# Other loads, fold engines and order for the first stage of an FFT-and-MLP kernel

## The chip, the cores and the metric

The kernel runs on one core of a Trainium2 chip. The metric is the device time of one execution in microseconds (us), and a kernel's time is the median of several runs. Profiles come from one more execution, recorded by the hardware profiler; their times count from the start of its span.

## The reference

The input x has 8 batches of 3008 rows of 256 columns, in f32. Each batch goes through a Fourier transform over its rows and one over its columns, and the real part is kept. The resulting 24064 rows are then the tokens of a two-layer MLP with a hard-swish between its layers:

```python
X = np.fft.fft(x, axis=1)              # (8, 3008, 256)
X = np.fft.fft(X, axis=2).real.astype(np.float32)
t = X.reshape(24064, 256)
h = t @ w_in                           # 256 x 2048
g = h * np.clip(h + 3.0, 0.0, 6.0) / 6.0
out = g @ w_out                        # 2048 x 256
```

## The kernel before

**The work and its stages.** The transform over 3008 = 47 x 64 rows is done in two stages of matrix products with constant tables, 47 points (table `F`) and 64 points (table `T`). The column transform is a table `C`, which is folded into `w_in` (the products of L860), so that it costs no stage of its own. Then come the two products of the MLP: L566 gives `u` and `v`, ScalarE and VectorE make the hard-swish of them (L575 to L617), and L641 and L661 multiply by `w_out` and gather the sums `acc`. L724 to L727 (`send`) store the result. The batches run one behind the other in an order fixed by hand: the program is recorded under a manual schedule, so each engine's queue holds its instructions in the order of the source. The body of the kernel is a long sequence in which stage one and two of the next batches are threaded between the MLP products of this one; the change does not touch it, apart from which moment the first pieces of it begin.

**Stage one of the first batch.** This is the part that the change rewrites. It has no MLP work beside it, since nothing has been transformed yet. It runs in four units, m = 0, 1, 3, 2 (`FIRST`), and each unit in two parts. Part 0 works on a forward tile `hb.x[m]`, part 1 on a reverse tile `hb.xr[m]`. A tile has 128 partitions of 4 consecutive rows of x (4 x 256 f32, 4 KB a partition), so 512 KB; 47 + 47 of the partitions hold what is computed on, the halves starting at partitions 0 and 64 (`PB` = 64, `XC` = 4). In both kernels the reverse tiles are read by an indirect gather on GpSimd's queue (L175), by a list of row numbers that `iota` makes; in the kernel before, so are the forward tiles, the two kinds in turn.

Each part is first folded, since a real transform over columns needs only sums and differences of a column and its mirror: columns 129 to 255 of `y` become differences (L203), columns 1 to 127 sums (L212), and columns 0 and 128 are copied (L209 on ScalarE, L214 on VectorE). TensorE then multiplies `y` by the table in four quarters (two halves of rows by two of columns, 47x512, L347 and, one slot at a time, L352), and the middle column of the raw tile by two more tables (`unit_middle`, L335). In the kernel before, part 0 of the first two units is different: TensorE sums near and far columns itself, in products of 258 and 254 columns from the raw tile (`unit_by_pe`), and VectorE makes only the differences (`sine`). A unit's sums are copied out of PSUM (`evict_first`, L365 to L367), sent to a scratch array `zd` in DRAM, and read back regrouped for stage two (L447, `g<-zd`).

**The weights.** `w_in` and `w_out` come in pieces of 512 KB (`load_w`, L769 to L774): the pieces 0 and 1 are of `w_in`, 2 and 3 are of `w_out`, and so on in turn. Each piece j is taken apart on chip into a scaled form by `exponent_a` (ScalarE, L790), `exponent_b` (TensorE, L804), `exponent_c` (ScalarE, L807), `mantissa` (VectorE, L815 and L816) and `join` (VectorE, L824 and L830). `fold_w_in` then multiplies a piece of `w_in` by `C` (L860), copies it out, and `send_wn` (L847) sends part of it through DRAM.

**Order around the start, before.** SyncE's queue holds the table `FI` and piece 0. ScalarE's holds `F`, `first_slot` (48 partitions of 1 KB, for the one slot that has no row of its own) and, after the first unit, piece 1. GpSimd's holds the eight gathers, `C`, two tables `T` and pieces 2 and 3. `exponent_a` and `mantissa` of piece 0 stand ahead of the units on their engines, its `exponent_b` and `exponent_c` behind the first unit's part 0. `keep_awake` (L887) issues filler products of 128x512 on constants, four of them before the first tile.

The stores of `send` serve as a comparison in the prediction. Their DRAM side is written in three dimensions, `rows[:, q].rearrange("b i e -> i b e")`, and their SBUF side is the tile `o` with 128 partitions.

Of the kernel before, what the change touches and what calls it, by code (L numbers as in the profile page):

```python
# [58 lines left out]
def kernel(  # L59
# [10 lines left out]
    nc = tc.nc  # L70
# [108 lines left out]

    class Half:  # L180
# [20 lines left out]
    def fold_columns(x, y, part, js, eng):  # L201
        far, near = x[0:PX - 1, js, D - 1:P:-1], x[0:PX - 1, js, 1:P]
        eng.tensor_tensor(y[:, js, P + 1:D], *((far, near) if part else (near, far)), op=AL.subtract)  # L203
        return near, far

    def fold_all(x, part, eng, steps=(slice(0, XC),), copy=None):
        y = ypool.tile([PX - 1, XC + 1, D], F32, tag="y", name="y")
        if copy:
            copy(y[:, 0:XC, 0:P + 1:P], x[0:PX - 1, :, 0:P + 1:P])  # L209
        for js in steps:  # L210
            near, far = fold_columns(x, y, part, js, eng)
            eng.tensor_tensor(y[:, js, 1:P], near, far, op=AL.add)  # L212
            if not copy:
                eng.tensor_copy(y[:, js, 0:P + 1:P], x[0:PX - 1, js, 0:P + 1:P])  # L214
        return y
# [116 lines left out]
    def unit_middle(m, part, x, pt, open_, close):  # L332
        for i, h, js, slots, alone in quarters(m, part):
            t = (1 + part) if alone else (5, 7)[part]
            nc.tensor.matmul(pt[h][i * PB:(i + 1) * PB, js], table(t, h), x[rows(h), slots, P:P + 1], start=open_ and not alone, stop=close,  # L335
                             skip_group_check=True)

    def unit_columns(m, part, src, ps, to, fr, open_, close, only=None):
        for i, h, js, slots, alone in quarters(m, part):
            parts = [(to, fr)]  # L340
            if alone and (to.start or 0) <= P < to.stop - 1:
                parts = [(slice(0, P + 1), slice(0, P + 1)), (slice(P + 1, D), slice(P + 1, D))]
            for a, b in parts:
                t = (1 + part + 2 * (a.start > P)) if alone else (0, 6)[part]
                o = ps[h][i * PB:(i + 1) * PB, js, a]
                if only is None:
                    nc.tensor.matmul(o, table(t, h), src[rows(h), slots, b], start=open_ and not alone, stop=close, skip_group_check=True)  # L347
                    continue
                js_, sl = range(js.start, js.stop), range(XC)[slots]
                for jj, ss in zip(js_, sl):  # L350
                    if jj == only:
                        nc.tensor.matmul(ps[h][i * PB:(i + 1) * PB, jj:jj + 1, a], table(t, h), src[rows(h), ss:ss + 1, b],  # L352
                                         start=False, stop=close, skip_group_check=True)

    def unit_by_pe(m, part, x, sine, ps, open_):
        unit_columns(m, part, x, ps, slice(0, P + 1), slice(0, P + 1), open_, False)
        unit_columns(m, part, x, ps, slice(1, P), slice(D - 1, P, -1), False, False)
        unit_columns(m, part, sine, ps, slice(P + 1, D), slice(P + 1, D), False, False)

    def evict_first(hb, m, ps, pt):  # L360
        k = FIRST.index(m)
        pool, tag = ((zpool, "z"), (zpool, "z"), (apool, "a"), (cpool, "c"))[k]
        z = pool.tile([PX, 2, 2, D + 1], F32, tag=tag, name="z")
        for h in range(2):
            nc.scalar.copy(z[:, h, :, D:], pt[h][0:PX])  # L365
        nc.scalar.copy(z[:, 0, :, 0:D], ps[0][0:PX])
        (nc.vector.tensor_copy if k == NM - 1 else nc.scalar.copy)(z[:, 1, :, 0:D], ps[1][0:PX])  # L367
        if not first.zd:
            first.zd[0] = dpool.tile([NG, 2 * KK, 2, NS, D + 1], F32, tag="zd0", name="zd")
        zd = first.zd[0][:].rearrange("g k c (h n) d -> (g k c) h (n d)", h=2)  # L370
        n0 = 2 * 4 * KK
        for i in range(2):
            n = (m * XC + 2 * i) * (D + 1)
            for j in range(PZ // n0):
                dst = zd[j * n0:(j + 1) * n0, :, n:n + 2 * (D + 1)]
                rs = slice(i * PB + j, i * PB + 2 * n0, 2) if j < 2 else slice(i * PB + 2 * n0, i * PB + PZ)
                src = z[rs].rearrange("p h n d -> p h (n d)")
                if j == 0:
                    (nc.scalar if k == NM - 1 and i else nc.sync).dma_start(out=dst, in_=src)
                else:  # L380
                    later.setdefault((j, k), []).append((dst, src))
# [377 lines left out]
    def load_w(j):  # L759
# [5 lines left out]
        if kind == "in":  # L765
            c0, c1 = in_columns(n, i)
            for h, cs in enumerate((slice(c0, c1 + P),) if n else (slice(c0, c0 + P), slice(c1, c1 + P))):
                nf = cs.stop - cs.start
                (nc.sync, nc.scalar, nc.gpsimd)[min(j, 2)].dma_start(  # L769
                                    out=o.rearrange("p (c j) -> p c j", c=2)[:, :, h * P:h * P + nf],  # L770
                                    in_=moe_w_in[:, cs].rearrange("(c p) f -> p c f", p=P))
# [20 lines left out]
    def exponent_b(j, own=False):  # L792
        pm = [PM[j % len(PM)][:, i].bitcast(F16) for i in range(2)]
        if (starting[0] or j == 4) and not own:
# [54 lines left out]
    def fold_w_in(j):  # L849
# [12 lines left out]
        if n == 0:  # L862
            o = W1[:].rearrange("p b (h f) -> p b h f", h=2)[:, :, :, c0:c0 + P]
            nc.vector.tensor_copy(o, ps[:].rearrange("p b (h f) -> p b h f", h=2))
# [18 lines left out]
    def keep_awake(n, ps=None):  # L883
        if ps is None:
            ps = ps_d.tile([P, 2 * TB], F32, tag="d", name="awake")
        for i in range(n):
            nc.tensor.matmul(ps[:], ones[:], Z[:], start=True, stop=True)  # L887
# [11 lines left out]
    for k, m in enumerate(FIRST):  # L899
        take_half(hb, m, *((xpool, "x"), (xpool, "x"), (qpool, "q"), (apool, "a"))[k])  # L900
# [36 lines left out]
    for i in range(2):  # L937
# [11 lines left out]
    for j in range(2, 4):  # L949
        load_w(j)  # L950
    clear_table(0)
    exponent_a(0)
    mantissa(0)
    clear_table(1)
    every = slice(0, D)

    def fold_unit(k, part):
        x = (hb.xr if part else hb.x).pop(FIRST[k])
        if k < 2 and part == 0:
            sine = cpool.tile([PX - 1, XC, D], F32, tag="c", name="sine")  # L960
            fold_columns(x, sine, 0, slice(0, XC), nc.vector)
            return x, sine
        steps = (slice(1, XC, 2), slice(0, XC, 2)) if k == NM - 1 and part else (slice(0, XC),)
        return x, fold_all(x, part, nc.vector, steps, nc.scalar.copy if k > 1 else None)

    unit = fold_unit(0, 0)
    for k, m in enumerate(FIRST):
        ps, pt = first_banks(m)
        x, y = unit
        if k == 0:  # L970
            unit_middle(m, 0, x, pt, True, False)
        if k < 2:
            unit_by_pe(m, 0, x, y, ps, True)
        else:
            unit_columns(m, 0, y, ps, every, every, True, False)
        if k == 0:
            exponent_b(0)
            exponent_c(0)
        else:
            unit_middle(m, 0, x, pt, True, False)  # L980
        x, y = fold_unit(k, 1)
        unit_middle(m, 1, x, pt, False, True)
        if k < NM - 1:
            unit_columns(m, 1, y, ps, every, every, False, True)
            unit = fold_unit(k + 1, 0)
        else:
            for j in range(2):
                unit_columns(m, 1, y, ps, every, every, False, True, only=j)
            join(0)
        evict_first(hb, m, ps, pt)  # L990
        if k == 0:
            nc.scalar.copy(zero_slot(hb), first_slot[PB:PX, 0:D])
            load_w(1)
# [3 lines left out]
    seen = wpool.tile([P, 1], F32, tag="seen", name="seen")  # L997
    mantissa(1)
    fold_w_in(0)
    exponent_a(1)  # L1000
    keep_awake(1)
    exponent_b(1)
    exponent_a(2, (0,))
    exponent_c(1)
    exponent_a(2, (1,))
    join(1)
    mantissa(2)
# [6 lines left out]
    exponent_b(2)  # L1014
    exponent_a(3, (0,))
    exponent_c(2)
    exponent_a(3, (1,))
    mantissa(3)
    fold_w_in(1)
    join(2)  # L1020
    stage2_half(hb, 0)
    exponent_b(3)
    spread_by_pe(hb, bank([P, TB], "ps3")[:])
    tail(3)
# [77 lines left out]
    uv = mlp1_products(*chunk(0))  # L1102
    activate(*chunk(0), *uv)
    ps = spare[0]
# [198 lines left out]
```

## Time and profile before

| | |
|---|---|
| median of 3 runs | 1935.53 us (1935.20 to 1935.71) |
| the profiled execution, its own time | 1933.92 us |
| its span | 1932.2 us |
| mean granted clock of TensorE | 0.997 |
| VectorE, ScalarE, GpSimd busy | 74%, 35%, 75% of the span |
| moved by DMA | 99.03 MB, 51 GB/s over the span |
| DMA in the first 24 us | 56% of 16 engines' time to 4 us, then 98 to 102% |
| L661, the second product of the MLP | 1238.9 us of PE |
| L566, the first product of the MLP | 777.1 us of PE |

PE is TensorE and PEld its weight loads, which lie beside the products. A line of a timeline gives start, length, engine, line of the kernel, operation, output and inputs with their shapes, the count, and in brackets the idle time before it with what ended that. A line of the windows gives, for each engine, the busy time and the number of instructions, then the clock that was granted to TensorE (1.00 is full speed), the share of the 16 DMA engines' time that was used, and GB/s. In the DMA view a queue's line gives packets, MB, and the share of 16 engines. SPq, ACTq and POOLq are the queues by which SyncE, ScalarE and GpSimd issue transfers.

The busy times of L661 and L566 add up to more than the span because products are pipelined and one's record overlaps the next's.

### The profile page before, as it was taken

To read this page: it belongs to the slowest core of one execution; us is meant where nothing else is said; L and a number is where in the kernel's file an instruction comes from. 1 tells how busy PE (TensorE), PEld (TensorE's weight loads), DVE (VectorE), ACT (ScalarE), POOL (GpSimd) and SP (SyncE) were. 2 spreads that over 40 slices of the span, in tenths; PEclk is the share of its full clock that TensorE was granted. 3 is DMA by queue.
4 is the path that set the end of the run, shared out by engine and by line. 5 is a ranking of instruction groups with operands and counts; after the bars stand their busy time and mean duration, and the time that the engine had idled before them with its cause. 6 is when DMAs were issued, how large, how long until landed. Compare 5 with 4: busy or idle time off the path is not lost.

```text
span 1932.2 us, 28221 instructions
## 1 busy us (share of the span) xinstructions
PE 1915.4 (99%) x9354; PEld 1650.8 (85%) x9354; DVE 1425.0 (74%) x2752; ACT 679.3 (35%) x1168; POOL 1442.7 (75%) x1653
## 2 busy tenths in 40 slices
PE   8999999999999999999999999999999999999998
PEld 5688888888988888888898888888899888888887
DVE  6877776677777777777787777777778777777777
ACT  6543333333333333333333333333333333333332
POOL 4597888896688778787678877878666667666765
PEclk9999999999999999999999999999999999999999
DMA  8431232311112222121111221121110101101000
GB/s 286 122 87 49 56 83 72 64 44 38 32 33 67 62 53 55 44 54 34 31 36 50 52 55 44 52 53 50 36 28 20 28 17 27 33 14 28 18 21 20
DMA packets 155592, 99.03 MB, mean 51 GB/s; under 512 B 122163, under 2 KB 137246, under 8 KB 155446
## 3 DMA queue, kind: packets, MB, share of 16 engines
q1 hardware_dynamic: 142582, 57.63, 12.4%
q0 software_dynamic: 11168, 38.51, 6.8%
q8 instruction: 73, 1.20, 0.3%
q10 hardware_dynamic: 1696, 1.10, 0.2%
q14 instruction: 73, 0.60, 0.1%
HBM read 59.87 MB, written 37.32 MB: 50 GB/s over the span
## 4 chain that ended last, share of the span: by engine, by line
PE 96%; DVE 2%; ACT 1%; DMA 0%; issue 0%; another core or an unknown queue 0%; SPq 0%; DVEq 0%; ACTq 0%
PE acc L661 57%; PE v L566 17%; PE u L566 16%; PE ps L514 2%; PE acc L641 1%; PE ps L287 1%; DVE a L617 1%; PE spare L860 1%; DVE s L575 0%; ACT t L614 0%; DVE o L722 0%; PE ps L475 0%; DVE u L598 0%; DMA st<-in_moe_w_in_dram 0%; PE wps L860 0%
## 5 line engine op out<-in xcount | busy, mean ns | idle before, releaser
L631 POOL TENSOR_TENSOR c<-a 128x512 f32<-128x512 f32 (+1 forms) x375 | 469.0, 1251 | 360.3 <-PE acc L661 310.5
L661 PE MATMUL acc<-c,G 128*128 128x256 f32 (+1 forms) x3008 | 697.2, 375 | 0.0
L614 ACT ACTIVATE t<-u,half 128x512 f32<-128x512 f32 (+1 forms) x384 | 260.5, 678 | 1144.2 <-DVE u L585 1062.4
L661 PEld LDWEIGHTS acc<-c,G 128*128 128x128 f32 x3008 | 565.3, 190 | 71.5 <-POOL c L631 0.4
L575 DVE SCALAR_TENSOR_TENSOR s<-qn,WN,u 128x256 f32<-128x256 f32 (+1 forms) x768 | 330.2, 471 | 339.3 <-PE u L566 336.7
L661 PE MATMUL acc<-a,G 128*128 128x256 f32 (+1 forms) x2256 | 541.7, 376 | 0.0
L661 PEld LDWEIGHTS acc<-a,G 128*128 128x128 f32 x2256 | 421.0, 189 | 73.6 <-issue 20.2
L566 PE MATMUL v<-q,W 127*128 127x256 f32 (+1 forms) x1536 | 389.2, 375 | 1.6 <-DVE a L617 1.3
L566 PE MATMUL u<-q,W 128*128 128x256 f32 (+1 forms) x1536 | 387.9, 375 | 0.0
L617 DVE SCALAR_TENSOR_TENSOR a<-t,u 128x512 f32<-128x512 f32 (+2 forms) x448 | 263.9, 601 | 102.5 <-ACT t L614 99.4
L566 PEld LDWEIGHTS v<-q,W 127*128 127x128 f32 x1536 | 287.9, 190 | 42.0 <-ACT t L614 2.2
L566 PEld LDWEIGHTS u<-q,W 128*128 128x128 f32 x1536 | 285.8, 190 | 36.9 <-issue 2.4
L631 POOL TENSOR_TENSOR c<-a,c 128x256 f32<-128x256 f32 (+1 forms) x375 | 268.5, 716 | 29.4
L631 POOL TENSOR_TENSOR c<-c,a 128x256 f32<-128x256 f32 (+1 forms) x375 | 268.4, 716 | 29.4
L585 DVE TENSOR_TENSOR u<-s,v 128x512 f32<-128x512 f32 x352 | 245.0, 696 | 38.1 <-DVE s L575 1.9
L617 DVE SCALAR_TENSOR_TENSOR a<-t,v 128x512 f32<-128x512 f32 (+1 forms) x480 | 263.1, 564 | 0.2
L614 ACT ACTIVATE t<-v,half 128x512 f32<-128x512 f32 (+1 forms) x384 | 260.4, 678 | 0.6 <-issue 0.4
L587 DVE TENSOR_TENSOR v<-v,s 128x512 f32<-128x512 f32 x352 | 243.7, 692 | 0.0
L631 POOL TENSOR_TENSOR r<-w,e 128x256 f32<-128x256 f32 (+1 forms) x92 | 88.8, 986 | 3.6
L671 ACT ACTIVATE e<-acc 128x512 f32<-128x512 f32 (+2 forms) x184 | 83.3, 544 | 0.0
L722 DVE STREAM_TRANSPOSE o<-r 128x256 f32<-128x256 f32 (+1 forms) x192 | 72.5, 414 | 0.2
L631 POOL TENSOR_TENSOR w<-w,e 128x512 f32<-128x512 f32 (+1 forms) x46 | 57.5, 1251 | 3.6
(127 smaller groups left out, 773.2 us busy)
## 6 DMA issues: line engine op xcount, KB each, us to landing
out_dram<-o SPq DMA_DIRECT2D x744, 32.0 KB
g<-zd SPq DMA_DIRECT2D x42, 256.0 KB
zd<-z SPq DMA_DIRECT2D x48, 192.0 KB
xt<-in_x_dram POOLq DMA_DIRECT2D x21, 256.0 KB, 3.7
st<-in_moe_w_out_dram POOLq DMA_DIRECT2D x8, 512.0 KB, 6.6
qn<-qd SPq DMA_DIRECT2D x16, 256.0 KB
xt<-in_x_dram POOLq DMA_DIRECT2D x17, 192.0 KB, 4.0
st<-in_moe_w_in_dram POOLq DMA_DIRECT2D x6, 512.0 KB, 4.9
```

Source lines behind the costliest of these rows:

```text
L287: nc.tensor.matmul(ps[b][h * PB:(h + 1) * PB, 0:n], F[rows(b), 0:PB], y[rows(b), 2 * h:2 * h + n], start=True, stop=not last, skip_group_c ...
L514: nc.tensor.matmul(ps[:, blk, u * P:n].rearrange("p (b k) -> p b k", b=2), g[:, kk, blk * (P + 1):blk * (P + 1) + P], T[:, :, gr, blk, kk, ...
L566: nc.tensor.matmul(ps[:, i, 0:nq], W1[r, blk, f * P:(f + 1) * P], q[r, blk, of:of + nq], start=True, stop=True)
L575: nc.vector.scalar_tensor_tensor(s[:, i, 0:nq], qn[:, of:of + nq], WN[:, f:f + 1], u[:, i, 0:nq], op0=AL.mult, op1=AL.add)
L585: nc.vector.tensor_tensor(u[:], s[:], v[:], op=AL.add)
L587: nc.vector.tensor_tensor(v[:], v[:], s[:], op=AL.subtract)
L614: nc.scalar.activation(t, h, AF.Relu, bias=half[:], scale=scale)
L617: nc.vector.scalar_tensor_tensor(dst, t, 1.0, h, op0=AL.min, op1=AL.mult)
L631: (eng or nc.gpsimd).tensor_tensor(out, in0, in1, op=AL.add)
L661: nc.tensor.matmul(ch.acc[i // 2][:, i % 2, 0:ch.n], G[:, i, fc, :], mv, start=(fc == 0 and i % 2 == 0), stop=(fc == NF - 1), skip_group_c ...
L671: nc.scalar.mul(ch.e[:, k:i + 1, 0:ch.n], ch.acc[i // 2][:, 0:i + 1 - k, 0:ch.n], 1.0 / WS)
L722: nc.vector.transpose(o[:, 0:n // DH, h], ch.r[:, m, h, 0:n].rearrange("p (j i) -> p j i", i=DH))
```

## The change

- The four forward tiles of the first batch are no longer gathered. `load_rows` issues each as one plain load on SyncE's queue, ahead of all else on it. Its source is the 64 partitions' worth of rows of `x_pn` with one more dimension of two ahead of it, for the second half of the tile.
- Pieces 0 and 1 of the weights follow on the same queue. `FI` moves to ScalarE's queue, between `F` and `first_slot`. GpSimd's queue begins with the four reverse gathers.
- All units are folded alike (`fold_unit`), and `unit_by_pe` is gone. The differences of part 0 of units 1, 2 and 3 are taken by GpSimd. Pieces 2 and 3 are issued on GpSimd's queue behind the second of these.
- A filler product of 128 columns stands behind each of the first seven parts.
- The copies out of unit k - 1 stand behind part 0 of unit k, for the last of them within part 1 of the last unit, behind `exponent_a` of piece 0. The wider half of a copy out goes to VectorE for two units instead of one.
- `mantissa`, `exponent_b`, `exponent_c` and `join` of piece 0 move behind stage one. `fold_w_in(1)` and the `exponent_b`, `exponent_c` and `join` of piece 3 move behind the first `u` and `v`. Some of the filler products between them are moved or made narrower.

The core of the diff:

```diff
+    def load_rows(o, m, queue):
+        a = x_pn[0:PB, m * XC + 1:(m + 1) * XC + 1, :].rearrange("p n d -> p (n d)")
+        queue.dma_start(out=o[:].rearrange("p n d -> p (n d)"),
+                        in_=bass.AP(a.tensor, a.offset, [[NM * XC * D, 2], *a.ap]))
...
+    def fold_unit(x, part, steps=(slice(0, XC),), copy=nc.scalar.copy, sine=nc.vector):
         y = ypool.tile([PX - 1, XC + 1, D], F32, tag="y", name="y")
...
+            copy(y[:, js, 0:P + 1:P], x[0:n, js, 0:P + 1:P])
+            far, near = x[0:n, js, D - 1:P:-1], x[0:n, js, 1:P]
+            sine.tensor_tensor(y[:, js, P + 1:D], *((far, near) if part else (near, far)), op=AL.subtract)
+            nc.vector.tensor_tensor(y[:, js, 1:P], near, far, op=AL.add)
...
     keep_awake(4)
+    keep_awake(1, TB)
     hb = halves[0]
-    nc.sync.dma_start(out=FI[:], in_=c_stage1[:, 13 * PB:])
-    load_w(0)
+    for k, m in enumerate(FIRST):
+        take_half(hb, m, *((xpool, "x"), (xpool, "x"), (qpool, "q"), (apool, "a"))[k])
+        load_rows(hb.x[m], m, nc.sync)
+    for j in range(2):
+        load_w(j)
     nc.scalar.dma_start(out=F[:], in_=c_stage1[:, 0:8 * PB])
+    nc.scalar.dma_start(out=FI[:], in_=c_stage1[:, 13 * PB:])
...
-        if i == 0:
-            gather(hb.x[FIRST[0]], IT[:, NM + FIRST[0]:NM + FIRST[0] + 1], P, D)
-    for m in FIRST:
-        if m != FIRST[0]:
-            gather(hb.x[m], IT[:, NM + m:NM + m + 1], P, D)
-        gather(hb.xr[m], IT[:, m:m + 1], P)
+        if i:
+            for m in FIRST:
+                gather(hb.xr[m], IT[:, m:m + 1], P)
...
     for k, m in enumerate(FIRST):
         ps, pt = first_banks(m)
-        x, y = unit
...
+        end = k == NM - 1
+        for part, tiles in enumerate((hb.x, hb.xr)):
+            x = tiles.pop(m)
+            if end and part:
+                y = fold_unit(x, 1, (slice(1, XC, 2), slice(0, XC, 2)), copy=nc.vector.tensor_copy)
+                exponent_a(0)
+                evict_first(hb, FIRST[k - 1], *before)
+                unit_middle(m, 1, x, pt)
+                for j in range(2):
+                    unit_columns(m, 1, y, ps, only=j)
+                continue
+            y = fold_unit(x, part, copy=nc.scalar.copy if k + part else nc.vector.tensor_copy,
+                          sine=nc.gpsimd if k > 0 and part == 0 else nc.vector)
+            if k == 2 and part == 0:
+                for j in range(2, 4):
+                    load_w(j)
+            unit_columns(m, part, y, ps)
+            unit_middle(m, part, x, pt)
+            keep_awake(1, P)
+            if part == 0 and k > 0 and not end:
+                evict_first(hb, FIRST[k - 1], *before)
+            if k == 1 and part == 0:
+                nc.scalar.copy(zero_slot(hb), first_slot[PB:PX, 0:D])
+        before = ps, pt
+    evict_first(hb, m, *before)
...
+    keep_awake(1)
+    mantissa(0)
+    exponent_b(0)
+    exponent_c(0)
+    keep_awake(1)
+    join(0)
     mantissa(1)
+    exponent_a(1)
+    mantissa(2)
     fold_w_in(0)
...
     uv = mlp1_products(*chunk(0))
+    exponent_b(3)
+    exponent_c(3)
     activate(*chunk(0), *uv)
+    fold_w_in(1)
+    join(3)
```

More of the change, by code (lines that the diff above doesn't have):

```diff
@@ L330, in quarters, with unit_middle @@
                     yield i, h, slice(1, 2), slice(XC - 1, XC) if part == 0 else slice(0, 1), True
-    def unit_middle(m, part, x, pt, open_, close):
+    def unit_middle(m, part, x, pt):
         for i, h, js, slots, alone in quarters(m, part):
             t = (1 + part) if alone else (5, 7)[part]
-            nc.tensor.matmul(pt[h][i * PB:(i + 1) * PB, js], table(t, h), x[rows(h), slots, P:P + 1], start=open_ and not alone, stop=close,
-                             skip_group_check=True)
-    def unit_columns(m, part, src, ps, to, fr, open_, close, only=None):
-        for i, h, js, slots, alone in quarters(m, part):
[L340 to L358, printed above, removed]
+            nc.tensor.matmul(pt[h][i * PB:(i + 1) * PB, js], table(t, h), x[rows(h), slots, P:P + 1],
+                             start=part == 0 and not alone, stop=part == 1, skip_group_check=True)
@@ new lines, in unit_columns, with product @@
+    def unit_columns(m, part, y, ps, only=None):
+        def product(o, t, h, moving, begin):
+            nc.tensor.matmul(o, table(t, h), moving, start=begin, stop=bool(part), skip_group_check=True)
+        for i, h, js, slots, alone in quarters(m, part):
+            o = ps[h][i * PB:(i + 1) * PB]
+            if alone and only in (None, 1):
+                for k, cs in enumerate((slice(0, P + 1), slice(P + 1, D))):
+                    product(o[:, js, cs], 1 + part + 2 * k, h, y[rows(h), slots, cs], False)
+            elif not alone and only is None:
+                product(o[:, js], (0, 6)[part], h, y[rows(h), slots], part == 0)
+            elif not alone:
+                for j, slot in zip(range(js.start, js.stop), range(XC)[slots]):
+                    if j == only:
+                        product(o[:, j:j + 1], (0, 6)[part], h, y[rows(h), slot:slot + 1], False)
@@ L366, in evict_first @@
         nc.scalar.copy(z[:, 0, :, 0:D], ps[0][0:PX])
[L367 removed]
+        (nc.vector.tensor_copy if k > 1 else nc.scalar.copy)(z[:, 1, :, 0:D], ps[1][0:PX])
         if not first.zd:
@@ L793, in exponent_b @@
         pm = [PM[j % len(PM)][:, i].bitcast(F16) for i in range(2)]
-        if (starting[0] or j == 4) and not own:
+        if (starting[0] or j in (3, 4)) and not own:
             exs[j] = ps_h.tile([P, WB], F32, tag="uv", name="ex")[:]
@@ L934, in see @@
         nc.gpsimd.tensor_copy(seen[:], x)
-    for i in range(2):
+    for i in range(1, -1, -1):
         for h in range(2):
@@ L948 @@
     load_t(0, queue=nc.gpsimd)
[L949 to L964, printed above, removed]
@@ L966 @@
-    unit = fold_unit(0, 0)
+    for b in range(2):
+        clear_table(b)
     for k, m in enumerate(FIRST):
         ps, pt = first_banks(m)
-        x, y = unit
[L970 to L993, printed above, removed]
+        end = k == NM - 1
[22 more added lines that the diff above has]
+        before = ps, pt
@@ L1013 @@
     load_half(halves[1], ORDER[0])
[L1014 to L1017, printed above, removed]
+    join(2)
     mantissa(3)
-    fold_w_in(1)
-    join(2)
     stage2_half(hb, 0)
-    exponent_b(3)
     spread_by_pe(hb, bank([P, TB], "ps3")[:])
-    tail(3)
+    exponent_a(3)
     starting[0] = False
```

34 lines of the change are left out of this document (10 added, 24 removed).

## The prediction

> **What bounds the kernel now.** I read the page first, busy time and the chain that ended last.
>
> ```profile
> PE 1915.4 (99%) x9354; PEld 1650.8 (85%) x9354; DVE 1425.0 (74%) x2752; ACT 679.3 (35%) x1168; POOL 1442.7 (75%) x1653
> PE 96%; DVE 2%; ACT 1%; DMA 0%; issue 0%; another core or an unknown queue 0%; SPq 0%; DVEq 0%; ACTq 0%
> ```
>
> TensorE is the bound, and nothing that the change touches lies late in the span. So the change is worth the shift that it gives to the moment from which PE never waits again. That moment is in PE's own timeline of the first 100 us:
>
> ```profile
> 17.18 1.10 PE L347 MATMUL ps<-y,F 47*64 47x512 f32 x12 [1.46 <-ACT y L209]
> ...
> 21.97 1.99 PE L352 MATMUL ps<-y,F 47*64 47x256 f32 x16
> ...
> 43.63 1.99 PE L860 MATMUL spare<-wi,C 128*128 128x256 f32 x8 [0.27 <-DVE wi L824]
> ...
> 71.33 1.13 PE L566 MATMUL v<-q,W 127*128 127x256 f32 x4 [0.72 <-DVE a L617]
> ```
>
> The reader is to see two marks. Stage one of the first batch ends at 23.96 (L352, 21.97 + 1.99). The fold of a weight piece at 43.63 is the last wait but one; after it PE loses 0.72 us once, at 71.33. From 23.96 to 43.63 are 19.7 us. The windows by 2 us add the clock of stage one's end:
>
> ```profile
> 16.00:18.00 2.00, 0.82 (x11) 0.69 (x15) 2.00 (x4) 1.15 (x5) 0.00 (x0) 1.00 0.98 300
> 18.00:20.00 2.00, 2.00 (x42) 1.69 (x38) 1.51 (x3) 0.65 (x4) 0.00 (x0) 0.75 1.05 269
> 20.00:22.00 2.00, 2.00 (x26) 0.84 (x27) 1.83 (x5) 1.00 (x3) 0.00 (x0) 0.50 1.04 367
> ```
>
> After a stretch in which PE was busy 0.82 of 2 us, half the clock was granted (0.50). The last column but one is the share of the 16 DMA engines: full all through. So stage one is paced by transfers, and the load that the change rewrites is the place to look.
>
> **How many engines a transfer uses.** The DMA view, first for 0 to 6 us, then 6 to 16, then 111 to 116:
>
> ```profile
> q10 hardware_dynamic: 208, 0.31, 16.7%
> ...
> F<-in_c_stage_dram ACTq DMA_DIRECT2D x1, 256.0 KB
> ...
> first_slot<-in_x_dram ACTq DMA_DIRECT2D x1, 48.0 KB
> ```
>
> ```profile
> DMA packets 1009, 3.62 MB, mean 362 GB/s; under 512 B 116, under 2 KB 129, under 8 KB 1009
> q0 software_dynamic: 994, 3.60, 98.7%
> ```
>
> ```profile
> DMA packets 1070, 0.29 MB, mean 58 GB/s; under 512 B 1056, under 2 KB 1056, under 8 KB 1070
> q1 hardware_dynamic: 1070, 0.29, 25.6%
> ```
>
> SyncE's timeline names what was issued just before and in it:
>
> ```profile
> 110.05 4.77 SPq L727 DMA_DIRECT2D out_dram<-o  x8
> ```
>
> The first answer holds two transfers on ScalarE's queue, F of 128 rows and first_slot of 48: 176 rows, and 208 packets. The 32 more are end marks, 16 for each: both used all 16 engines. The third answer holds eight stores of `send`, 128 pieces of 256 bytes each, whose destination is nested 4 x 32 x 64 while their source is 128 rows. 8 x 128 = 1024, and 1056 packets are under 512 bytes: 32 marks, four a store. Those stores ran on four engines, and no slice of that answer is above 74 GB/s while they run alone. So a plain transfer is spread over no more engines than the outermost count of its coarser side allows: 16 for 128 or 48 rows, 4 for 4.
>
> The new load has 128 rows on the SBUF side, but its source is written as `[[NM * XC * D, 2], *a.ap]`, 2 x 64 rows of 4 KB. By the stores' row that is **two engines**.
>
> [...]
>
> **The change, part by part.**
>
> *The loads.* A packet of 4 KB costs an engine: 98.7% of 16 engines' 10 us over some 880 packets (994 less the marks) = 0.18 us. At the best slice of that answer (475 GB/s, 29.7 per engine) it is 0.138; the fullest microsecond (12 to 13: 110.2%, 93 packets) gives 0.19. I take 0.16, between, since with two engines busy the memory is not contended. A tile is 64 packets on each of the two, four tiles 256: 256 x 0.16 = 41.0 us (35.3 to 48.4). The same two engines also carry a sixteenth each of F, FI, first_slot, the four reverse gathers, C and T, 3.02 MB: 188 KB, 46 packets, 7.4 us (6.4 to 8.7), and of the two w_out pieces, 16 packets, 2.6 us (0 if these come later, up to 3.0). First bytes move at 1.8 us. The fourth tile lands at 1.8 + 41.0 + 7.4 + 2.6 = 52.8 us (43.5 to 61.9). Before, all eight tiles had been used by 21.9.
>
> *Weights behind x.* Piece 0 stands behind the four tiles on SP's queue, so on those two engines it comes last: 32 KB on each, some 1.3 us. ScalarE's first `exponent_a` waits for it, and the copy of unit 2's middle column, queued behind it, releases the last unit's products. From the fourth tile that is 1.3 + 1.45 (L790, two) + 0.22 = 3.0 us.
>
> *The last two units.* POOL's difference of 128x508 costs 1.26 (L226's row), then PE's products and middle column 1.4 at full clock, and 2.4 at half (21.58 to 23.96). At half clock: 1.3 + 2.5 + 0.4 (filler) + 2.4 = 6.6 us from the fourth tile to the end of stage one; at full clock the weights' path decides, 3.0 + 1.5 = 4.5. PE would sit idle some 8 us for every pair of units, and 1.46 us of idling was enough before to lose the clock, so I take 6.6. Stage one ends at 52.8 + 6.6 = **59.4, which is 35.4 later** than 23.96.
>
> *Three differences on POOL.* They take three times 0.69 off VectorE and put three times 1.26 on POOL. The w_out loads 2 and 3 queue behind the second difference, and with it behind the third tile. Nothing here is late next to the tiles: nothing, with the landing as cover; without it 1.26 a unit.
>
> *PE's own work.* Two units lose 254 of 766 columns a quarter, about 0.4 us each. Seven fillers of 128 columns cost a quarter of L887's 0.86, 1.5 us together, in stretches where PE waits; of three wider ones (0.86, 0.86, 0.43) behind stage one, one took the place of an old one.
>
> *The steps behind stage one.* On PE, by rows: filler, exponent, filler, 0.3 for the join, fold 1.73, two exponents and a filler 1.3, stage two 0.89, spread 0.46: 6.9 us to the first u. Then u and v 1.73, exponent 0.43, fold 1.73, half a stage two 0.95, u and v 1.73, two halves of acc 3.44, two exponents 0.87: 17.8 us to the fold that was at 43.63, against 19.7. At half clock for the first 6 us, until PE has been busy long enough, 2 more: 19.8. So nothing is given or taken here (-1.9 to +3).
>
> **Sum.** +35.4 us on the span, 1967.6, and 1.7 us around it as in the profiled execution before (1933.92 against 1932.2). The median of the runs shown, 1935.53, stands 1.6 above that execution; I count from the median: 1935.5 + 35.4 = 1971.
>
> **The rivals.**
>
> *All 16 engines take the load (0.12).* For it: the SBUF side is 128 plain rows, and the gathers of the same bytes use 16. Against it: the stores, whose SBUF side is 128 plain rows too. The price: W1 of before was issued at 13.92 and moved nothing until 17, so transfers go about in the order of issue. F, FI, the slot, four forward tiles, W0, W1 and the gathers are 5.63 MB; at 0.35 MB/us the last gather lands at 17.9. The last unit then follows the one before it on PE, at 20.7, and stage one ends at 22.0 at full clock: 2.0 earlier, and 1.9 from the shorter steps behind, -3.9 us, 1931.6. It decides from the point where a tile takes under about 2 us to land. This sits on the border of what a measurement of this kernel can tell from no change, about 0.2% or 3.9 us, so I split it: 0.07 faster, 0.05 the same.
>
> *Two engines, but in the order of issue, with the reverse tiles behind (0.18).* The forward tiles then land by 43.4, but the first reverse tile's share of the two engines only at about 45, and seven units run one after another, the first few at half clock (2.6 us each), the rest at 1.45: stage one ends at 60 to 64, +38, 1973.5. For it: W1 above. Against it: the gathers come from another queue, and in 4 to 5 us both queues moved bytes side by side.
>
> *Two engines, in turn (0.70):* the sum above, 1971.
>
> **The numbers.** Low end: the cheapest packet, w_out later, the clock kept: 43.5 + 4.5 = 48.0, +24.0 - 1.9 = +22, 1957.5. High end: the dearest packet, 61.9 + 6.9, and 3 more behind: +48, 1983.5. Faster 0.07, same 0.05, slower 0.88.
>
> **What would show it.** Right: tiles landing about 10 us apart; a DMA share near 2/16 and some 50 GB/s between 20 and 50 us; PE idle until each forward tile, with VectorE's and POOL's folds waiting on xt from DMA; PE's clock at 0.5 for most of it; the last stage-one product near 59; the fold of L860 near 79, and from there the old course, 35 us later. Wrong: four tiles down by 10 us and a full DMA share.

## The result, and the profile after

The changed kernel takes 1982.18 us (median of 4 runs, 1981.72 to 1982.84) against 1935.60 for the kernel before, beside it. The ratio is 1.0241, 95% interval 1.0224 to 1.0259: 46.6 us slower. Its profiled execution took 1981.72 us with a span of 1980.0, 47.8 longer than before. First its page, busy time and chain:

```profile
PE 1928.8 (97%) x9342; PEld 1657.9 (84%) x9342; DVE 1428.9 (72%) x2752; ACT 681.0 (34%) x1170; POOL 1443.7 (73%) x1652
PE 93%; DMA 3%; DVE 2%; SPq 1%; ACT 0%; issue 0%; POOL 0%; DVEq 0%; ACTq 0%; POOLq 0%
```

TensorE is still the bound, but DMA and SyncE's queue have come into the chain with 4%, all of it at the start. PE's timeline of the changed kernel (start, length, engine and line, operands, count, idle time before):

```profile
25.18 1.98 PE L339 MATMUL ps<-y,F 47*64 47x512 f32 x8 [17.50 <-DVE y L213]
...
35.73 1.98 PE L339 MATMUL ps<-y,F 47*64 47x512 f32 x8 [4.98 <-POOL y L212]
...
45.05 1.98 PE L339 MATMUL ps<-y,F 47*64 47x512 f32 x8 [6.51 <-ACT y L210]
...
47.80 1.99 PE L339 MATMUL ps<-y,F 47*64 47x512 f32 x12
...
60.39 1.98 PE L339 MATMUL ps<-y,F 47*64 47x512 f32 x8 [5.91 <-POOL y L212]
...
63.37 1.96 PE L339 MATMUL ps<-y,F 47*64 47x256 f32 x16
...
89.84 3.45 PE L853 MATMUL spare<-wi,C 128*128 128x256 f32 x8 [3.57 <-DVE wi L817]
```

The four parts with a forward tile begin at 25.18, 35.73, 47.80 and 60.39, 10.6 to 12.6 us apart. The line at 45.05 is part 1 of the second unit. Its reverse tile had long landed, but ScalarE's copy for it (L210) stands behind the copy of `first_slot` into the third tile (L967), and that waited for the third tile until 44.37. Stage one ends at 65.33 (63.37 + 1.96), 41.4 later than before. The fold (now L853) comes at 89.84, 46.2 later, and takes 3.45 instead of 1.99. With it the 47.8 us are all there: 41.4 to the end of stage one, 4.8 more to the fold, 1.5 in it.

The DMA view of 24 to 34 us, and the windows around it (busy time of PE, PEld, DVE, ACT, POOL, then clock, DMA share, GB/s):

```profile
DMA packets 130, 0.52 MB, mean 52 GB/s; under 512 B 2, under 2 KB 2, under 8 KB 130
...
q1 hardware_dynamic: 130, 0.52, 12.8%
```

```profile
24.00:34.00 10.00, 5.57 (x36) 2.60 (x36) 2.45 (x5) 0.16 (x1) 0.10 (x1) 0.50 0.13 52
34.00:44.00 10.00, 2.82 (x18) 1.30 (x18) 2.81 (x3) 1.25 (x5) 1.67 (x1) 0.50 0.23 78
```

In ten microseconds 128 packets of 4 KB and two end marks: one tile, at 12.8% of sixteen engines, which is two of them, and 52 GB/s. The trace also holds landing marks, events at the end of a load: sixteen for each of the reverse gathers, two for each of these tiles, read here as one from each engine that carried a share. By these the tiles were down at 23.74, 33.74, 44.29 and 58.41. A 4 KB packet took 159 ns (here and below the median of the packets of that size in the window). The reverse gathers show who else was on the two engines: fourteen marks of the first were there by 7.36, its last two at 11.28 and 11.82. The clock is at 0.50 from 11.7 to 69.7.

Behind stage one there is a new wait. VectorE's timeline, then SyncE's and GpSimd's issues:

```profile
86.00 0.48 DVE L568 SCALAR_TENSOR_TENSOR s<-qn,WN,u 128x256 f32<-128x256 f32 x1 [3.08 <-DMA WN<-W]
87.32 0.48 DVE L568 SCALAR_TENSOR_TENSOR s<-qn,WN,u 128x256 f32<-128x256 f32 x1 [0.83 <-DMA WN<-W]
```

```profile
72.40 7.95 SPq L840 DMA_DIRECT2D WN<-W  x4
```

```profile
74.79 1.49 POOL L762 DMA_DIRECT2D st<-in_moe_w_in_dram  x2
76.25 1.46 POOL L767 DMA_DIRECT2D st<-in_moe_w_out_dram  x2
77.69 1.46 POOL L762 DMA_DIRECT2D st<-in_moe_w_in_dram  x2
```

The second fold of a weight piece, moved behind the first `u` and `v`, is copied out at 78.5 to 79.1 and then sent through DRAM, just when six weight pieces (3 MB) have been issued. By their landing marks the two sends of it, issued at 79.09 and 79.60, took 6.8 and 7.7 us. VectorE needs them at once, waits 3.08 and 0.83, PE idles 3.57 and loses its clock (0.50 from 90.2 to 93.6). In the kernel before, the same two sends went out at 32.30 and 32.81, beside the same pieces, and took 6.4 and 7.3 us. But they were down at 40.15, and VectorE's line that uses them has no wait:

```profile
40.73 0.87 DVE L575 SCALAR_TENSOR_TENSOR s<-qn,WN,u 128x256 f32<-128x256 f32 x2
```

So the round trip was slow in both kernels; the move took away the time between a send and its use.

### The profile page after: what moved, and what is told of

Same layout as the page of the kernel before. It is cut to its first block, busy times and chain, and to the rows that moved or that the text cites. A ratio compares the mean times of both kernels' runs of the same rounds, so it can differ in the third digit from the quotient of the medians.

```text
span 1980.0 us, 28209 instructions
## 1 busy us (share of the span) xinstructions
PE 1928.8 (97%) x9342; PEld 1657.9 (84%) x9342; DVE 1428.9 (72%) x2752; ACT 681.0 (34%) x1170; POOL 1443.7 (73%) x1652
## 4 chain that ended last, share of the span: by engine, by line
PE 93%; DMA 3%; DVE 2%; SPq 1%; ACT 0%; issue 0%; POOL 0%; DVEq 0%; ACTq 0%; POOLq 0%
PE acc L654 55%; PE v L559 16%; PE u L559 16%; DMA xt<-in_x_dram 2%; PE ps L507 2%; PE acc L634 1%; PE ps L286 1%; SPq L182 1%; PE spare L853 1%; DVE a L610 1%; DVE s L568 0%; DMA WN<-W 0%; ACT t L607 0%; DVE o L715 0%; PE ps L468 0%; DVE u L591 0%
```

## The experiments

One theory for the 41 us (the load runs on two engines) and one for the rest (the fold's round trip) stood against the order of the queues, the folds on GpSimd and the weights behind x. The table sums up all runs: where stage one ended, when the fold came that was at 43.63, and the median. a_rows and b_rows ran once each, the others four to ten times.

| run | end of stage one | the fold | median, us |
|---|---|---|---|
| before | 23.96 | 43.63 | 1935.6 |
| after | 65.33 | 89.84 | 1982.2 |
| a_split | 33.22 | 57.87 | 1950.4 |
| a_rows | 52.08 | 76.62 | 1970.0 |
| a_fold | 65.54 | 87.69 | 1977.7 |
| b_rows | 78.18 | 99.16 | 1990.2 |
| split_fold | 33.05 | 55.45 | 1945.9 |
| split_awake | 28.83 | 52.65 | 1944.9 |
| best1 | 36.39 | 57.48 | 1948.7 |
| b_awake | 20.70 | 40.13 | 1931.2 |
| split_both | 29.03 | 50.12 | 1939.3 |
| hw8 | 30.35 | 50.99 | 1942.2 |
| a_gather | 34.06 | 58.06 | 1951.2 |
| hw8_128 | 26.22 | 46.89 | 1937.6 |

The kernel before, run beside them, had medians of 1934.96 (first four), 1935.01 (next four), 1935.23 (next three) and 1933.36 (the last).

**a_split: the same rows, another nest.** In these lines a loop over row ranges, which here has one range for each half, is written out.

```diff
-        queue.dma_start(out=o[:].rearrange("p n d -> p (n d)"),
-                        in_=bass.AP(a.tensor, a.offset, [[NM * XC * D, 2], *a.ap]))
+        for h in range(2):
+            queue.dma_start(out=o[h * PB:(h + 1) * PB].rearrange("p n d -> p (n d)"),
+                            in_=bass.AP(a.tensor, a.offset + h * NM * XC * D, [*a.ap]))
```

> The changed kernel, each forward tile loaded by two plain transfers of 64 rows (one for each half) instead of one whose source is nested 2 x 64. Theory (a transfer is spread over no more engines than the outermost count of its coarser side allows): the four tiles land by about 14 us instead of 58.4, stage one ends between 21 and 25 instead of 65.3, and the time falls by some 41 us, to 1935 to 1941 (the upper end if the 6 us lost behind stage one stay). Rival (the order of the queues, the folds on GpSimd or the weights behind x hold it): within 3 us of 1982. Second rival (SyncE's queue is slow for such loads in any form): tiles still 5 us or more apart, over 1955.

1950.38 us, ratio to before 1.0077 (1.0060 to 1.0094). The first rival falls: with order, folds and weights untouched, 31.8 us went. The second (tiles 5 us or more apart, over 1955) falls too, but not by far: the tiles were down at 8.26, 12.45, 16.75 and 21.08, some 4.3 us apart, where the theory had the last at about 14. And 1950 lies above its 1935 to 1941, and stage one ended at 33.2, not 21 to 25. The windows show why:

```profile
8.64:12.05 3.41, 1.57 (x18) 0.81 (x18) 2.37 (x4) 0.52 (x2) 0.09 (x1) 1.00 1.05 255
12.05:15.46 3.41, 3.36 (x22) 1.69 (x26) 1.60 (x3) 0.21 (x1) 1.76 (x1) 0.50 1.04 264
```

Two things were not foreseen: the engines are full (1.05) but move only 255 GB/s, where the gathers of before moved 383 from 8 to 12, and PE, kept waiting, lost its clock at 12.05.

**a_rows: other row counts.** The halves of the four tiles, in order, as 62 + 2, 64, 60 + 4 and 51 + 13 rows.

```diff
+        step, ends = a.ap[0][0], {0: (62, PB), 1: (PB,), 3: (60, PB), 2: (51, PB)}[m]
+        for h in range(2):
+            for r0, r1 in zip((0, *ends), ends):
+                queue.dma_start(...)   # rows r0 to r1 of half h
```

> The changed kernel with every half tile loaded by two or one plain transfers of other row counts: first tile 62 + 2 rows, second 64, third 60 + 4, fourth 51 + 13. If the count of engines is the largest number up to 16 that divides the rows: 62 rows go over 2 engines, 64 over 16, 60 over 15, 51 over 3, to be read from the number of end marks of each transfer; the first tile then needs some 62 packets of 0.16 us on each of two engines, 10 us, more with the shares of other transfers, and lands near 17 to 23; the fourth needs 34 on each of three, 5.4 us. The time is some 10 to 20 us above that of the plain 64-row loads. If it is only the nest in the source that counts, all of these use 16 engines, and the time is that of the plain 64-row loads within 2 us.

1969.96 us, 19.6 above a_split. The landing marks of a transfer: 62 rows, two (14.47 and 15.90); 60 rows, fifteen; 51 rows, three (36.38, 36.77, 37.13). VectorE's first fold waited for the second 62 + 2:

```profile
26.79 0.17 DVE L213 COPY y<-xt 111x8 f32<-111x8 f32 x1 [23.59 <-DMA xt<-in_x_dram]
```

That is later than the 17 to 23 expected. From 20 to 26 us the DMA view has only two engines' worth of work (12.7%), and 39 of its 84 packets belong to the gathers: the two engines carried both. So it is not the nest as such: a plain source of 62 rows was as narrow as the nested one, with two marks. Two, fifteen and three marks are the counts that were expected for 62, 60 and 51 rows.

**a_fold: the moved fold put back.**

```diff
     mantissa(3)
+    fold_w_in(1)
     stage2_half(hb, 0)
...
     activate(*chunk(0), *uv)
-    fold_w_in(1)
     join(3)
```

> The changed kernel, its loads as they are, with the fold of piece 1 put back ahead of stage two and of the first u and v (behind the mantissa of piece 3). Theory: behind stage one 6 us were lost because the folded weights were sent at 79 to 80 us, behind six weight pieces, and VectorE waited for their return until 87.3; sent earlier they come in time, and the time falls by 4 to 7 us, to 1975 to 1978. Rival: what is late is the pieces and the traffic as a whole, wherever the fold stands: within 2 us of 1982.

1977.70 us (1977.57 to 1977.90), 4.5 less than the changed kernel, as expected. PE's line of the fold has no wait left:

```profile
87.69 1.99 PE L853 MATMUL spare<-wi,C 128*128 128x256 f32 x8
```

**b_rows: the nested loads alone, in the kernel before.** `FI` and piece 0 stay on SyncE's queue, now behind the tiles.

```diff
     hb = halves[0]
+    for k, m in enumerate(FIRST):
+        take_half(hb, m, ...)
+        load_rows(hb.x[m], m, nc.sync)     # nested 2 x 64
     nc.sync.dma_start(out=FI[:], in_=c_stage1[:, 13 * PB:])
     load_w(0)
...
-            gather(hb.x[FIRST[0]], ...)    # and the three other forward gathers
```

> The kernel before with one thing changed: the four forward tiles come by the nested loads of the change, first on SyncE's queue, in place of the gathers; all else as before. Theory: this load alone carries most of the change: 35 to 45 us slower than before, 1970 to 1980. Rival (it takes the other parts, the weights behind x or the folds on GpSimd, to make the loss): less than 10 us slower.

1990.15 us (one run), 55 above before: more than forecast. Its VectorE timeline says why:

```profile
59.35 0.43 DVE L820 TENSOR_SCALAR top<-st 128x512 int32<-128x512 int32 x1 [56.15 <-DMA st<-in_moe_w_in_dram]
```

In the kernel before, the mantissa of piece 0 stands ahead of every fold, and piece 0 now comes behind four slow tiles. No unit could be folded until 60. The change's own order, with that mantissa behind stage one, avoids this. So the load alone suffices for the loss, but this run doesn't give its size in the changed kernel.

**split_fold and split_awake: the two other costs, each alone, on top of the split loads.** The first is a_fold's edit. The second:

```diff
-    keep_awake(4)
+    keep_awake(5)
...
-            keep_awake(1, P)
+            keep_awake(1)
```

> The changed kernel with the loads split in 64 rows each, and the fold of piece 1 put back ahead of stage two. With the split loads alone stage one ends at 33.2, and VectorE still waits 3.4 and 0.9 us for the folded weights. Theory: the price of the moved fold doesn't depend on the tiles, so it comes off here as it did with the nested loads (4.5 us): 1945 to 1947. Rival: with early tiles the weights come late in any order, and it stays within 1.5 us of 1950.4.

> The changed kernel with the split loads, its seven fillers of 128 columns widened to 512, and one more of 512 ahead of the first tile. With the split loads alone PE was busy 1.57 of the 3.41 us before 12.05 and ran at half clock from there to 35.9. Theory (most of what the split loads left is the clock): the clock holds, stage one ends at 24 to 27 instead of 33.2, and the time falls by 5 to 9 us, to 1941 to 1945. Rival (the transfers, whose share is full until 28 us, set the pace of stage one, and PE's clock only fills the waits): within 2 us of 1950.4. Second rival (the fillers are in the way): above 1952.

split_fold: 1945.91 us (1942.04 to 1946.48), 4.5 less than a_split. split_awake: 1944.94 (1944.49 to 1945.96), 5.4 less, at the upper edge of what was forecast. The clock held (1.00 in every window from 0 to 40), and stage one ended at 28.8, not at 24 to 27. Its PE line has the full-clock duration (a_split 1.97):

```profile
27.76 1.07 PE L342 MATMUL ps<-y,F 47*64 47x256 f32 x16
```

**best1: the weights behind the gathers.** All of the above, and pieces 0 and 1 on GpSimd's queue.

```diff
-    for j in range(2):
-        load_w(j)
...
                 gather(hb.xr[m], IT[:, m:m + 1], P)
+            for j in range(2):
+                load_w(j)                  # on GpSimd's queue
```

> The changed kernel with split loads, wide fillers, the fold of piece 1 put back, and pieces 0 and 1 of the weights issued on GpSimd's queue behind the four reverse gathers instead of on SyncE's. Theory: the tiles then share the engines with no weights and land by about 17, stage one ends at 20 to 22 at full clock, and the steps behind it take some 20 us: 1930 to 1935, at or just below the kernel before. Rival (the plain loads and the gathers side by side move less a microsecond than gathers alone, 252 against 340 GB/s in 4 to 20 us): tiles land by 20 to 22, 1936 to 1941.

1948.67 us, ratio 1.0069 (1.0053 to 1.0086): both forecasts missed. GpSimd's timeline:

```profile
11.84 0.73 POOL L942 DMA_DIRECT2D C<-in_c_dim_dram  x1 [1.90 <-DMA xt<-in_x_dram,IT]
15.46 0.55 POOL L873 DMA_DIRECT2D T<-in_c_stage_dram  x1 [2.90 <-DMA xt<-in_x_dram,IT]
19.14 0.53 POOL L873 DMA_DIRECT2D T<-in_c_stage_dram  x1 [3.13 <-DMA xt<-in_x_dram,IT]
19.74 1.26 POOL L215 TENSOR_TENSOR y<-xt 111x508 f32<-111x508 f32 x1
```

Behind four gathers and four weight issues, each further issue waited until a gather had landed, and the difference of the second unit stands behind them. PE waited 5.83 us for it and lost the clock (0.53 from 20 to 24, 0.62 from 24 to 28).

**split_both, hw8 and a_gather: why the split loads are slow.** split_both joins split_fold and split_awake. hw8 is split_both with the reverse tiles, too, as plain 64-row loads on SyncE's queue. a_gather is the changed kernel with the forward tiles gathered as before.

```diff
 hw8:
+        load_rows(hb.xr[m], lambda h: (2 * NXC - 1 - h * NM - m) * XC, nc.sync)
...
-                gather(hb.xr[m], IT[:, m:m + 1], P)
 a_gather:
-        load_rows(hb.x[m], m, nc.sync)
...
+            gather(hb.x[m], IT[:, NM + m:NM + m + 1], P, D)
         gather(hb.xr[m], IT[:, m:m + 1], P)
```

> The changed kernel with the split loads, the wide fillers and the fold of piece 1 put back, each of which was tried alone. Theory (the wait for the folded weights and the clock are separate costs, 4.5 and 5.4 us): they add, 1940 to 1942. Rival (they hide each other): 1943.5 to 1945.

> As the run with split loads, wide fillers and the fold put back, but the four reverse tiles too are plain loads of 64 rows, in turn with the forward ones, all on SyncE's queue. A 4 KB packet took 159 ns on an engine in the kernel before (gathers alone) and in the changed kernel from 24 to 34 us (the nested loads alone), but 250 to 263 ns from 8 to 12 us with split loads beside gathers. Theory (two queues with 4 KB packets on one engine slow each other): with one queue the packets are back at 159 to 170 ns, the last tile lands by 17 to 19 instead of 21 to 22, and the time falls by 3 to 6 us against its neighbour, to 1935 to 1938. Rival (plain 64-row loads are slow in themselves): packets stay above 220 ns, and the time is within 1.5 us of its neighbour or above.

> The changed kernel with one thing undone: the four forward tiles are gathered again on GpSimd's queue, in turn with the reverse ones, as before the change. All else of the change stays (weights 0 and 1 alone on SyncE's queue, differences on GpSimd, narrow fillers, the moved steps). Theory: the loads carry all of the loss but some 5 to 10 us; packets at 159 to 190 ns, last tile by 18, stage one ends at 22 to 28 by the state of the clock, the wait for the folded weights stays: 1938 to 1946, below the split loads (1950.4), since here only one queue carries 4 KB packets. Rival (the split loads had already brought all that the loads can): 1949 to 1952.

split_both: 1939.25 us (1938.82 to 1940.60), ratio 1.0018 (1.0009 to 1.0028). It is 11.1 below a_split, slightly more than 4.5 + 5.4, and just below the 1940 to 1942 that was forecast: the two costs add, and do not hide each other.

hw8: 1942.22 (1940.09 to 1945.47), no faster than split_both, and packets of 298 ns with one queue on the engines: the theory of two queues falls. a_gather: 1951.16, ratio 1.0079 (1.0062 to 1.0096), no better than a_split, as its rival said, although its eighth tile was down at 19.4, as before (19.3). The start was late. The first tile was down at 9.44, in the kernel before at 7.07; two weight pieces on SyncE's queue go beside it, not one, but that this is the reason was not tested. And the first product waited for the fold of that tile until 10.87, where before it came at 7.12, straight from the raw tile. PE was busy 1.13 of the 4 us from 8 to 12, and from then on stage one ran at half clock (0.50 in each window from 12 to 32), to 34.06. So undoing the load in either way gives 31 to 32 us, and what is left in a_gather is not the landing of the last tile but the late start and the clock. The DMA views of 12 to 16 us, of hw8 and then of a_gather:

```profile
DMA packets 285, 0.92 MB, mean 229 GB/s; under 512 B 61, under 2 KB 61, under 8 KB 285
...
q1 hardware_dynamic: 285, 0.92, 104.3%
```

```profile
DMA packets 453, 1.65 MB, mean 412 GB/s; under 512 B 51, under 2 KB 51, under 8 KB 453
...
q0 software_dynamic: 453, 1.65, 102.9%
```

Same packet size, engines full in both, and 229 against 412 GB/s.

**hw8_128: one load of 128 rows.**

```diff
-        for h in range(2):
-            queue.dma_start(out=o[h * PB:(h + 1) * PB]...,
-                            in_=bass.AP(a.tensor, first_row(h) * D, [*a.ap]))
+        queue.dma_start(out=o[:].rearrange("p n d -> p (n d)"),
+                        in_=bass.AP(a.tensor, first_row(0) * D, [[step, P], *row]))
```

> As the run with all eight tiles by plain loads of 64 rows on SyncE's queue, but each tile is one plain load of 128 rows, 64 KB apart in DRAM as before; the upper half of each tile then holds other rows of x than the reference wants. Bytes, packet size, queue and order stay, the number of transfers halves. The 64-row loads, alone on the engines from 12 to 16 us, took 298 ns a packet and moved 229 GB/s; the gathers, which span all 128 partitions, 159 ns and up to 412 GB/s. [...] Rival (plain loads of rows 64 KB apart are slow by themselves, on the DRAM side or in their descriptors): packets stay above 250 ns and the time within 2 us of 1942. [...]

In this kernel the upper half of each tile holds other rows of x than the reference wants, so it serves as a measurement alone. It took 1937.62 us (1937.21 to 1938.36), ratio 1.0017 (1.0007 to 1.0027), where hw8 had 1.0037 (1.0025 to 1.0050). The medians of the two are 4.6 us apart. But the kernel before ran 1.9 us faster beside this run than beside hw8 (1933.36 against 1935.23), and the intervals overlap, so the gain in time is not settled. What the run settles is the transfer. The last tile was down at 17.21, in hw8 at 26.34. Its DMA view of the same window:

```profile
DMA packets 454, 1.64 MB, mean 411 GB/s; under 512 B 50, under 2 KB 54, under 8 KB 454
...
q1 hardware_dynamic: 454, 1.64, 102.6%
```

A packet took 161 ns instead of 298, and 229 GB/s became 411, with queue, packet size and pitch in DRAM unchanged, so the rival, packets above 250 ns, falls. Here loads into 64 partitions moved about half of what loads into 128 did, with sixteen engines full in both (104.3% and 102.6%). The run shows the halving; whether it lies in the 64 partitions or in twice as many transfers of half the size was not shown.

**b_awake: a better kernel.** The kernel before, with one filler and an earlier piece 1.

```diff
+            if k == 2:
+                keep_awake(1)
             unit_columns(m, 0, y, ps, every, every, True, False)
...
         gather(hb.xr[m], IT[:, m:m + 1], P)
+    load_w(1)                              # on GpSimd's queue
...
         if k == 0:
             nc.scalar.copy(zero_slot(hb), first_slot[PB:PX, 0:D])
-            load_w(1)                      # on ScalarE's
```

> The kernel before with two things: a filler of 512 columns ahead of part 0 of the third unit, where PE sat idle 1.46 us, and piece 1 issued on GpSimd's queue behind the gathers (before: on ScalarE's after the first unit, issued at 13.92 and landed at 25.8). Theory: the clock is not lost at 19.0, stage one ends at 21 to 22 instead of 24.0, and piece 1 is there by then: 2 to 4 us faster than before, about 1932. Rival (stage one is paced by the transfers, and piece 1 delays them): no faster, within 1.5 us of before.

1931.22 us (1930.19 to 1932.29, 10 runs), ratio 0.9979 (0.9970 to 0.9989): 3.8 us faster than the kernel before. Its PE line at the end of stage one and its window there, where the kernel before stood at 0.50:

```profile
19.60 1.10 PE L352 MATMUL ps<-y,F 47*64 47x256 f32 x16
```

```profile
20.00:24.00 4.00, 3.91 (x28) 2.32 (x20) 2.81 (x5) 2.30 (x5) 0.00 (x0) 1.00 0.82 300
```

Which of the two edits brought how much was not separated by a run. The landing marks give a hint: the eighth tile was down at 16.95 instead of 19.27, so of the 3.3 us by which stage one ends earlier 2.3 came with the tiles, and 0.9 behind the last of them, at full clock. The prediction had read the kernel before as paced by transfers. The marks bear that out as far as that tile; the 4.7 us behind it ran at half clock.

## Why the prediction was right

The direction, the mechanism and the range held; the middle was 11 us short (35.4 forecast, 46.6 measured, 47.8 in the spans). That the range held has some luck in it: 1982.2 lies 1.3 us below its high end, and the steps behind stage one lie outside the bounds that they were given there. It held because the last landing, 58.4, stayed 3.5 below its own high end. By its own steps:

- **Two engines**: right, with the numbers it named: tiles 10 us apart, a share of 0.13, 52 GB/s, the clock at 0.50, folds waiting on `xt`. The two marks of time came later than it said, the last product at 63.37 (near 59) and the fold at 89.84 (near 79). That all four tiles go over the same two engines, on which the 41.0 and the 10.0 count, no run shows, since no record names an engine. The trace shows two marks for each tile, and for the first half of piece 0, issued behind the tiles, fourteen marks by 42.96 and the last two at 58.12 and 59.08, around the fourth tile's 58.41.
- **256 packets of 0.16 us**: right, 159 ns, while a tile is alone on the engines. No run shows the reason given, memory that is not contended: the gathers before had the same 159 from 6 to 16 us, with sixteen engines busy 98.7%.
- **The other transfers on the same two engines, 10.0 us**: mis-sized. Landing was 58.4 instead of 52.8. From the first byte to the first tile went 21.9 us, where the two alone-running tiles took 10.0 and 10.6: 11.7 for the others, against 7.4. The packets of 4 to 10 us took 199 (gathers) to 219 ns (the loads) instead of 160. The last tile took 14.1, 3.9 more than a tile alone, against 2.6. Why packets beside each other cost more was not separated.
- **6.6 us from the fourth tile to the end of stage one**: 6.9. PE's half clock decided, not the weights: the exponents of piece 0 ended at 61.2.
- **GpSimd's differences, 1.26 each**: 1.76 beside a working VectorE. In the second and third unit the wait for the next tile hid that, as forecast. In the last unit the difference stands on the path, as the 6.6 had it, and cost 0.5 more than the 1.3 counted there.
- **The steps behind stage one, -1.9 to +3**: wrong, +6.3. The 6 us at half clock that it counts were 4.4 (0.50 to 69.73), and that being busy for long enough brings the clock back is not shown. The step costed the moved fold by PE's time alone. It left out that its result goes through DRAM, that this takes 6 to 8 us beside the weight pieces, and that behind the move VectorE needs it within 4 us, for the second `s`. a_fold took 4.5 of it back. By its own demand that each DMA of a moved step be counted against what it is moved past, this was to be found.
- **The rival of sixteen engines, 1931.6**: never tested as it stood, but its price was wrong: runs that had the tiles on sixteen engines came to 1950 and 1951. It assumed the full clock at once, and for plain loads the rate of the gathers.
- **The rival of two engines in the order of issue, 1973.5**: nearer to the time than the sum's 1971, but wrong in what it says: the four reverse tiles were all down by 20.46, before the first forward tile.

So the 46.6 us are some 31 from the load's nest, 11 from the fold's round trip and the clock in stage one (both measured with the split loads in place), and about 4 that remain in split_both (ratio 1.0018), where stage one still ends 5 us later than before.

## What to carry to other kernels

Before costing a load by its bytes, read its access pattern, the outermost count on each side and the partitions that it covers. Here 2 x 64 rows went over two engines, which cost 31 us, and plain loads of 62, 60 and 51 rows had two, fifteen and three landing marks. Loads of 64 rows into 64 partitions kept sixteen engines full (104.3%) and still moved only 229 GB/s, where loads of 128 rows into 128 moved 411. A step that sends its result through DRAM must keep enough time before its consumer, here 6 to 8 us beside other transfers. And where PE must wait for transfers, fillers of full size in the wait can be worth more than their own time (5.4 us here).

## What was not expected of the hardware

- In a_split the clock did not come back when PE was merely busy. PE had no gap from 25.7 to 32.5, at half clock (0.50):

```profile
25.70:29.10 3.40, 3.40 (x28) 2.33 (x24) 1.66 (x7) 0.96 (x2) 0.01 (x1) 0.50 0.84 323
29.10:32.50 3.40, 3.40 (x38) 2.01 (x34) 0.51 (x1) 0.94 (x5) 0.00 (x0) 0.50 0.06 15
```

It came back at 35.9, after fillers of 128x512 (128*128) had begun at 33.15; until then the products were 47*64 with short fillers between. So 6.8 us without a gap, of small products, weren't enough here. PE was 46% (a_split) and 57% busy (before, 15.58 to 19.00) in the 3.4 us before it lost the clock. But it kept the clock through 3.4 us with 55% in split_both (9.26 to 12.68) and with 51% in hw8 (11.04 to 14.46), which held fillers of 128x512. So the busy share alone does not decide, and what does was not measured.

- GpSimd and VectorE held each other up at these folds. GpSimd's 111x508 difference takes 1.26 us with VectorE idle (best1), VectorE's 0.68. Side by side in the changed kernel, whichever started second lasted longer:

```profile
33.87 0.69 DVE L213 TENSOR_TENSOR y<-xt 111x508 f32<-111x508 f32 x1 [7.55 <-DMA xt<-in_x_dram]
33.90 1.77 POOL L212 TENSOR_TENSOR y<-xt 111x508 f32<-111x508 f32 x1 [25.18 <-DMA xt<-in_x_dram]
34.47 1.75 DVE L212 TENSOR_TENSOR y<-xt 111x508 f32<-111x508 f32 x1
```

GpSimd's ended 1.1 us after VectorE's first, and VectorE's second 0.55 after GpSimd's, close to what each takes alone. In a_gather GpSimd came first and took its 1.26, and VectorE's took 1.41.
